# Computing an attention output already transposed, in quadrants of 32 rows

## The chip, the cores and the metric

The kernel runs on one core of a Trainium2 chip. The metric is the time of one execution on the device in microseconds (us). Three runs of the kernel before gave 1435.74, 1436.57 and 1439.3 us; the median, 1436.57 us, is the time before.

## The reference

Three layers follow one another. The first is a gated linear attention over 4 batches, 8 heads, 768 steps and 48 channels; its output, with the heads side by side, is a matrix of 3072 tokens by 384 features. The other two are mixtures on each token.

```python
f = 1.0 / (1.0 + np.exp(-f_logit))
for t in range(S):
    state = f[:, :, t, :, None] * state + np.einsum('bhd,bhe->bhde', k[:, :, t], v[:, :, t])
    y[:, :, t] = np.einsum('bhd,bhde->bhe', q[:, :, t], state)
x = y.transpose(0, 2, 1, 3).reshape(B * S, H * D)
h = x @ w_in                                   # 384 -> 2048
g = (a0 + a1*h + a2*h**2 + a3*h**3) / (1 + abs(b0)*abs(h) + abs(b1)*h**2 + 1e-6)
x = g @ w_out                                  # 2048 -> 384
for e in range(4):                             # 384 -> 1024 -> 384
    out += p[:, e:e+1] * (np.maximum(x @ w1[e], 0) @ w2[e])
```

## The kernel before

The time axis is cut into six chunks of 128 steps, and each chunk into four blocks, one for each batch: 24 blocks. A block of attention works on four pairs of heads; a pair's two heads stand on partitions 0 to 47 and 64 to 111. All chunks of the first mixture after the first, and all of the second, multiply in a split form: a value is a high and a low part, and each product takes three matmuls of 512 columns (`mm_in`, line 836, and `mm_out`, line 846). These are called the main matmuls here. The attention itself uses plain f32, which the profile shows as two records for one product.

One block goes through these steps. Its scores are eight products of k and q, one for each head (`scores`, line 464); VectorE multiplies them by the mask into the two tiles am (`masked`, line 475). k is transposed (`k_t`, line 480) and copied by ScalarE. The output y, tokens on partitions and 384 features on columns, is summed in one bank: for each pair a product of q with the state (`inter`, line 493, weights q, 96 columns of state streaming), and for each head a product of am with v (`intra`, line 488, weights am, 48 columns of v streaming). ScalarE copies y out of the bank (`y_copy`, line 508), TensorE transposes it in three parts (`x_t`, line 511), and ScalarE copies the result into the first mixture's input x as its high part (`x_hi`, line 520); VectorE subtracts to get the low part (`x_lo`, line 525). In the meantime `update` (line 504) multiplies k and v, and `finish` (lines 527 to 538) renews the state for the next chunk. Chunk 0 has no `inter` and no low part.

The order of the work is written out by hand. `fused` walks over steps v; a step holds one expert slice of the second mixture (nine main matmuls in, nine out) and in some steps slices of the first mixture. `Att.stage` says what a block does in its steps k = 1 to 7, and `Att.t0` when a block begins. Two of its lists are fillers: PA is spread among the nine main matmuls of the slice's input product, PB among the nine of its output product (`fill_run` and `fill_step`, one entry of the list at a time). In chunks 1 to 5 the products for y are fillers of PB in step 5; the transposes x_t are fillers in step 6 (chunk 1) or 7 (later chunks). REST is what comes after the step's matmuls. The four blocks of chunk 0 go through `Att.first`, ahead of the second mixture, beside the conversion of the first mixture's weights on VectorE and ScalarE; after it, the first chunk's mixture is computed in f32 (`fill_in`, line 874, and `fill_out`, line 881). Loads of q, k, f and v go through SP's queue. v is loaded in step 2 of a block, 128 rows of 384 numbers.

Of the kernel before, what the change touches and what calls it, by code (L numbers as in the profile page):

```python
# [8 lines left out]
F32 = mybir.dt.float32  # L9
# [8 lines left out]
NB, NH, S, D = 4, 8, 768, 48  # L18
DM = NH * D
C = 128  # L20
NCH = S // C
NP = NH // 2
PR = 112
# [2 lines left out]
NJ2 = 8  # L26
NSLOT = NJ1 + NE * NJ2
SW = 2 * DM
RING = 16
CONV = (-6, -5, -4, -4, -3, -2, -2, -1, 0, 1, 2, 3, 4, 5, 6, 7)  # L30
WARM = (14, 3, 6)
# [307 lines left out]
PA, PB, ACT0, ACT1, POOL1, DVE1, REST = range(7)  # L339
# [57 lines left out]
class Block:  # L397


    def __init__(self, att, c, b):  # L400
        self.att, self.nc, self.c, self.b = att, att.tc.nc, c, b
        if c == 0:
            self.pa, self.pk, self.py = att.bank_sets[b % 2]
            self.px = self.pk
        elif c == 1:
            self.pa, self.pk, self.py = att.bank_sets[0]
            self.px = self.pk
        else:
            self.pa, self.py = self.pk, self.px = att.pair
        self.last = c == NCH - 1  # L410

    def load(self, i):
        t = self.att.p2.tile([128, NP, C], F32, tag="qkf"[i], name="qkf"[i])
# [1 line left out]
        setattr(self, "qkf"[i], t)  # L415

    def load_v(self):
        self.v = self.att.p2.tile([128, DM], F32, tag="v", name="v")
        self.nc.sync.dma_start(out=self.v, in_=self.att.aps["v"][self.b, self.c * C:(self.c + 1) * C, :])

    def exp(self):
# [61 lines left out]
        self.kt = self.att.p1.tile([128, NP, PR], F32, tag="kt", name="kt")  # L483
        self.nc.scalar.copy(out=self.kt, in_=self.pk.rearrange("p (r c) -> p r c", r=NP)[:, :, 0:PR])

    def intra(self, r, a):
        o = (2 * r + a) * D
        self.nc.tensor.matmul(self.py[:, o:o + D], self.am[a][:, r], self.v[:, o:o + D],  # L488
                              start=(self.c == 0 and r == 0 and a == 0), stop=(r == NP - 1 and a == 1))

    def inter(self, r):
        o = 2 * r * D
        self.nc.tensor.matmul(self.py[:, o:o + 2 * D], self.q[0:PR, r], self.att.st[self.b][0:PR, r],  # L493
                              start=(r == 0), stop=False)

    def y_parts(self, *rs):
        fs = []
        for r in rs:
            fs += ([partial(self.inter, r)] if self.c else []) + [partial(self.intra, r, a) for a in range(2)]
        return fs  # L500

    def update(self, r):
        o = 2 * r * D
        self.nc.tensor.matmul(self.pa[0:PR, o:o + 2 * D], self.kt[:, r], self.v[:, o:o + 2 * D], start=True, stop=True)  # L504

    def y_copy(self):
        self.y = self.am[0].rearrange("p r t -> p (r t)")[:, 0:DM]
        self.nc.scalar.copy(out=self.y, in_=self.py[:, 0:DM])

    def x_t(self, m):  # L510
        self.nc.tensor.transpose(self.px[:, m * C:(m + 1) * C], self.y[:, m * C:(m + 1) * C], self.att.consts[2])

    def x_part(self, i):
        x = self.att.x_of(self.c)
# [1 line left out]
        return x[:, :, self.b * C:(self.b + 1) * C]  # L516

    def x_hi(self):
        xt = self.px[:, 0:DM].rearrange("p (m t) -> p m t", m=3)
        self.nc.scalar.copy(out=self.x_part(0), in_=xt)  # L520

    def x_lo(self):
        if self.c:
            xt = self.px[:, 0:DM].rearrange("p (m t) -> p m t", m=3)
            self.nc.vector.tensor_tensor(out=self.x_part(1), in0=xt, in1=self.x_part(0).bitcast(F32), op=ALU.subtract)

    def finish(self):
# [13 lines left out]
class Att:  # L541
# [41 lines left out]
    def first(self, s, conv):  # L583

        new, old, nxt = (self.blocks.get((0, b)) for b in (s, s - 1, s + 1))
        rs = range(NP)
        if s == 0:
            new.exp()
            self.warm(WARM[0])
        if old:  # L590
            old.k_copy()
        if new:
            new.w()
            new.scans()
            new.inverse()
            new.k_hat()
        if nxt:
            nxt.exp()
        for f in conv[0]:
            f()  # L600
        if old:
            old.masked()
            for f in old.y_parts(*rs):
                f()
            for r in rs:
                old.update(r)
        if new:
            new.newton1()
            new.newton2()
            new.q_hat()  # L610
        if old:
            old.y_copy()
            for m in range(3):
                old.x_t(m)
            old.x_hi()
        if new:
            self.warm(WARM[1])
            for r in rs:
                new.scores(r)
            for r in rs:  # L620
                new.k_t(r)
            self.warm(WARM[2])
        for f in conv[1]:
            f()
        if old:
            old.finish()
        if s + 2 < NB:
            blk = self.blocks[0, s + 2] = Block(self, 0, s + 2)
            for i in (2, 1, 0):
                blk.load(i)  # L630
        if old and s + 1 < NB:
            self.blocks[0, s + 1].load_v()
# [14 lines left out]
    def stage(self, blk, k):  # L647
        rs = range(NP)
        if k == 1:
            return {ACT0: [blk.exp], DVE1: [blk.w], REST: [blk.scans]}  # L650
        if k == 2:
            return {ACT0: [blk.inverse], POOL1: [blk.k_hat], DVE1: [blk.newton1], REST: [blk.newton2]}
        if k == 3:
            return {POOL1: [blk.q_hat]}
        if k == 4:
            return {PA: [blk.all_scores] + [lambda: None] * (8 * (blk.c == 1)), REST: [blk.masked]}
        keys = [] if blk.last else [partial(blk.k_t, r) for r in rs]
        upd = [] if blk.last else [partial(blk.update, r) for r in rs]
        copy = [] if blk.last else [blk.k_copy]
        end = ([] if blk.last else [blk.finish]) + [blk.x_lo]  # L660
        xt = [partial(blk.x_t, m) for m in range(3)]
        if blk.c == 1:
            if k == 5:
                return {PB: keys + blk.y_parts(*rs), REST: copy}
            if k == 6:
                return {PA: upd, ACT1: [blk.y_copy], PB: xt, REST: [blk.x_hi] + end}
            return {}
        if k == 5:
            return {PB: keys + blk.y_parts(*rs), REST: copy}
        if k == 6:  # L670
            return {PA: upd, ACT1: [blk.y_copy]}
        if k == 7:
            return {PA: xt, ACT1: [blk.x_hi], REST: end}
        return {}

    def begin(self, v):
        ops = tuple([] for _ in range(7))
        for c in range(1, NCH):
            for b in reversed(range(NB)):
                k = v - self.t0(c, b)  # L680
                if 1 <= k <= 7:
                    for at, fs in self.stage(self.blocks[c, b], k).items():
                        ops[at].extend(fs)
        return ops
# [477 lines left out]
def gla_moe_kernel(tc, qkf, v, vt, w1, w2, ab, probs, ident_d, mask_d, out):  # L1162
    nc = tc.nc
    aps = {"qkf": qkf, "v": v, "vt": vt, "w1": w1, "w2": w2, "out": out}
    with (
# [14 lines left out]
        xs = dp.tile([DM, NB, S], F32, name="xs")  # L1180
# [35 lines left out]
        with tc.If(rv == 0, preferred_fallthrough_block=False):  # L1216
            scan_attention(tc, aps, xs)

            def load_x(g, dst):
                for m in range(3):  # L1220
                    nc.sync.dma_start(out=dst[:, m, :].rearrange("p (b t) -> p b t", b=NB),
                                      in_=xs[m * 128:(m + 1) * 128, :, g * C:(g + 1) * C])
            plain_ffn(tc, aps, consts, load_x)


# [3 lines left out]
def _pack(inputs):  # L1229
    import numpy as _np  # L1230

    def pairs(a, pad):
        a = a.reshape(NB, NP, 2, NCH, C, D).transpose(3, 0, 2, 5, 1, 4)
        return _np.concatenate([a, a[:, :, :, 0:16] if pad else _np.zeros_like(a[:, :, :, 0:16])], axis=3).reshape(
            NCH, NB, 128, NP, C)

    def slots(w_in, w_out):
        f = w_in.shape[1]
        n = f // 128
        a = w_in.reshape(3, 128, n, 128).transpose(2, 1, 0, 3).reshape(n, 128, DM)  # L1240
        return _np.concatenate([a, w_out.reshape(n, 128, DM)], axis=2)

    w1 = slots(inputs['moe_w_in'], inputs['moe_w_out'])
    w2 = [slots(inputs['moe2_w1'][e], inputs['moe2_w2'][e]) for e in range(NE)]
    return {
        'qkf': _np.stack([pairs(inputs['q'], 0), pairs(inputs['k'], 0), pairs(inputs['f_logit'], 1)], axis=3),
        'v': inputs['v'].transpose(0, 2, 1, 3).reshape(NB, S, DM),
        'vt': inputs['v'].transpose(0, 1, 3, 2),
        'w1': _np.ascontiguousarray(w1).view(_np.int64),
        'w2': _np.concatenate(w2, axis=0),  # L1250
        'ab': _np.tile(_np.concatenate([inputs['moe_a'], inputs['moe_b']])[None, :], (128, 1)),
        'probs': inputs['moe2_domain_probs'].reshape(NB, NCH, 128, NE).transpose(2, 1, 0, 3).reshape(128, NCH * NB, NE),
        'ident': _np.eye(128, dtype=_np.float32),
        'mask': _np.triu(_np.ones((128, 128), dtype=_np.float32)),
    }
# [23 lines left out]
```

## Time and profile before

| what | value |
| --- | --- |
| median of three runs | 1436.57 us |
| the profiled execution's own time | 1440.86 us |
| its span, first to last instruction | 1439.0 us |
| PE busy | 1378.3 us (96%) |
| weight loads (PEld) busy | 1105.8 us (77%) |
| VectorE (DVE) busy | 904.4 us (63%) |
| ScalarE (ACT) busy | 674.4 us (47%) |
| GpSimd (POOL) busy | 287.4 us (20%) |
| DMA | 287.80 MB, 200 GB/s |
| share of the chain that ended last | PE 75%, DVE 14%, DMA 3% |

PE stands for TensorE's matmuls and PEld for its weight loads, which overlap them. Matmuls are pipelined: the duration of one row contains its passage through the array, so the pitch between starts, not the duration, is what a matmul takes of a stream. A row with a count joins neighbours of one line; its duration runs from the first start to the last end. A bracket behind a row says how long the engine was idle before it and what ended that.

### The profile page before, as it was taken

Reading aid. Unit: us, or ns where it says so; the run is one execution under the profiler, and the core shown is the slowest. Engines: PE = TensorE matmul, PEld = TensorE weight load, DVE = VectorE, ACT = ScalarE, POOL = GpSimd, SP = SyncE. Lnnn points to the kernel's source line nnn. Section 1 sums busy time; section 2 is a strip of 40 time slices with the busy share of each in tenths; the row PEclk is TensorE's granted clock in tenths of the full one; section 3 lists DMA queues with packets and bytes.
Section 4 is the critical chain, followed back from the end, with each engine's and each line's share of the span. In section 5 each row is a group of like instructions: output and inputs, shape, how many; then the busy total and the mean of one; then the engine's idle time right before and its main releaser. Section 6 shows DMA issues by size and latency. Waiting matters only on the chain.

```text
span 1439.0 us, 18273 instructions
## 1 busy us (share of the span) xinstructions
PE 1378.3 (96%) x6502; PEld 1105.8 (77%) x6502; DVE 904.4 (63%) x1403; ACT 674.4 (47%) x1160; POOL 287.4 (20%) x257
## 2 busy tenths in 40 slices
PE   6898999898989999999999999999999999999996
PEld 6643688686878888887888887888878888888885
DVE  7799844968656657667556676657675655562222
ACT  3577545775635544445454444444444444441111
POOL 0123554556532101112001112001111001111010
PEclk8799999899999999999999999999999999999998
DMA  8244875576766655657566566656556666667650
GB/s 301 91 140 155 284 256 203 207 260 228 279 238 210 215 182 180 208 148 262 174 188 213 167 190 228 204 179 217 193 170 219 195 200 196 193 193 239 194 176 25
DMA packets 115699, 287.80 MB, mean 200 GB/s; under 512 B 13104, under 2 KB 31888, under 8 KB 114832
## 3 DMA queue, kind: packets, MB, share of 16 engines
q1 hardware_dynamic: 115024, 286.36, 61.6%
q8 instruction: 54, 0.88, 0.3%
q14 instruction: 45, 0.37, 0.1%
q10 hardware_dynamic: 576, 0.18, 0.0%
HBM read 237.69 MB, written 48.81 MB: 199 GB/s over the span
## 4 chain that ended last, share of the span: by engine, by line
PE 75%; DVE 14%; DMA 3%; ACT 2%; issue 2%; POOL 2%; SPq 1%; POOLq 0%; ACTq 0%; DVEq 0%
PE bank L846 34%; PE bank L836 32%; PE bank L488 2%; PE bank L464 1%; DMA f<-in_qkf_dram 1%; POOL w L793 1%; DVE y L931 1%; PE bank L493 1%; DVE g L434 1%; PE bank L881 1%; DVE q L910 1%; DVE q L905 1%; PE bank L504 1%; DVE q L919 1%; PE bank L874 1%
## 5 line engine op out<-in xcount | busy, mean ns | idle before, releaser
L836 PE MATMUL bank<-x,w 128*128 128x512 f32 x2448 | 609.2, 395 | 8.0 <-DVE gl L945 6.1
L846 PE MATMUL bank<-gh,w 128*128 128x512 f32 x1632 | 530.6, 401 | 6.0 <-DVE t L981 6.0
L836 PEld LDWEIGHTS bank<-x,w 128*128 128x128 f32 x2448 | 454.1, 189 | 103.0 <-DVE gl L945 7.8
L846 PEld LDWEIGHTS bank<-gh,w 128*128 128x128 f32 x1632 | 305.3, 190 | 68.4 <-DVE t L981 6.9
L846 PE MATMUL bank<-gl,w 128*128 128x512 f32 x816 | 324.9, 398 | 0.0
L945 DVE SCALAR_TENSOR_TENSOR gl<-bank,gh 128x512 fp32r<-128x512 f32 x192 | 131.7, 686 | 136.2 <-ACT gh L944 136.2
L982 POOL TENSOR_TENSOR o<-o,t 128x512 f32<-128x512 f32 x69 | 89.2, 1323 | 512.0 <-DVE t L981 512.0
L846 PEld LDWEIGHTS bank<-gl,w 128*128 128x128 f32 x816 | 154.5, 189 | 30.4
L944 ACT ACTIVATE gh<-bank 128x512 fp32r<-128x512 f32 x192 | 114.0, 594 | 125.9 <-PE bank L836 125.9
L910 DVE SCALAR_TENSOR_TENSOR q<-q,sc,r 128x512 f32<-128x512 f32 x80 | 62.7, 784 | 167.0 <-ACT r L895 167.0
L921 ACT CAST gh<-q 128x512 fp32r<-128x512 f32 x80 | 49.1, 614 | 160.9 <-DVE q L919 160.9
L793 POOL TENSOR_TENSOR w<-rawbuf,w 128x384 fp32r<-128x384 f32 x96 | 104.9, 1120 | 95.6 <-ACT w L792 66.7
L890 ACT COPY h<-bank 128x512 f32<-128x512 f32 x80 | 46.9, 586 | 137.5 <-PE bank L836 137.1
L999 DVE TENSOR_TENSOR s<-s,bank 128x512 f32<-128x512 f32 x45 | 30.7, 683 | 77.8 <-PE bank L846 77.8
L936 DVE TENSOR_TENSOR gl<-q,gh 128x512 fp32r<-128x512 f32 x80 | 55.3, 691 | 35.0 <-ACT gh L921 35.0
L488 PEld LDWEIGHTS bank<-v,am 128*128 128x128 f32 x384 | 65.0, 202 | 12.0 <-DVE am L475 7.9
L911 ACT ACTIVATE r<-q,sc 128x512 f32<-128x512 f32 x80 | 58.0, 725 | 30.9 <-DVE q L910 23.9
L488 PE MATMUL bank<-v,am 128*128 128x48 f32 x384 | 60.6, 264 | 7.5 <-DVE am L475 7.5
L905 DVE SCALAR_TENSOR_TENSOR q<-q,r 128x512 f32<-128x512 f32 x80 | 65.0, 812 | 0.0
L896 ACT ACTIVATE y<-h,sc 128x512 f32<-128x512 f32 x80 | 64.1, 801 | 0.0
L912 ACT ACTIVATE r<-r 128x512 f32<-128x512 f32 x96 | 60.7, 632 | 3.1
L931 DVE SCALAR_TENSOR_TENSOR y<-y,sc,h 128x512 f32<-128x512 f32 x80 | 60.2, 752 | 2.8
(103 smaller groups left out, 1393.3 us busy)
## 6 DMA issues: line engine op xcount, KB each, us to landing
w<-ws SPq DMA_DIRECT2D x448, 384.0 KB, 3.6
ws<-w SPq DMA_DIRECT2D x96, 384.0 KB, 4.1
raw<-in_w_dram SPq DMA_DIRECT2D x16, 768.0 KB, 7.0
rawbuf<-in_w_dram SPq DMA_DIRECT2D x64, 192.0 KB, 3.6
f<-in_qkf_dram SPq DMA_DIRECT2D x24, 256.0 KB, 3.9
k<-in_qkf_dram SPq DMA_DIRECT2D x24, 256.0 KB, 4.0
q<-in_qkf_dram SPq DMA_DIRECT2D x24, 256.0 KB, 4.2
w1s<-wf SPq DMA_DIRECT2D x16, 384.0 KB, 3.7
```

Of the source, the lines that this page charges most:

```text
L488: self.nc.tensor.matmul(self.py[:, o:o + D], self.am[a][:, r], self.v[:, o:o + D], start=(self.c == 0 and r == 0 and a == 0), stop=(r == N ...
L793: nc.gpsimd.tensor_tensor(out=t[:, 1], in0=r, in1=t[:, 0].bitcast(F32), op=ALU.subtract)
L836: nc.tensor.matmul(ps, a[:, o], b[:, kk, :], start=(n == 0), stop=(n == 8))
L846: nc.tensor.matmul(acc[m], a[:, o], b, start=(start and n == 0), stop=(stop and n == last))
L896: nc.scalar.activation(out=y, in_=h, func=AF.Identity, scale=sc[:, 0:1], bias=sc[:, 1:2])
L905: vec.scalar_tensor_tensor(out=q0, in0=q0, scalar=QC, in1=r0, op0=ALU.add, op1=ALU.mult)
L910: vec.scalar_tensor_tensor(out=q, in0=q, scalar=sc[:, 5:6], in1=r, op0=ALU.mult, op1=ALU.add)
L912: nc.scalar.activation(out=r, in_=r, func=AF.Exp, scale=-1.0)
L931: vec.scalar_tensor_tensor(out=y, in0=y, scalar=sc[:, 2:3], in1=h, op0=ALU.subtract, op1=ALU.mult)
L944: nc.scalar.activation(out=gh, in_=h, func=AF.Relu)
L945: nc.vector.scalar_tensor_tensor(out=gl, in0=h, scalar=0.0, in1=gh.bitcast(F32), op0=ALU.max, op1=ALU.subtract)
L982: nc.gpsimd.tensor_tensor(out=o[c][:, m], in0=o[c][:, m], in1=t, op=ALU.add)
```

## The change

The output is computed with features on partitions and tokens on columns. Now the state and v are the weights, and q and am stream. An output lies in column groups of 128 tokens (three of them, n), and in four quadrants of 32 partitions. Group n holds on partitions 0 to 95 the 96 features of pair n, and on partitions 96 to 127 the n-th third of pair 3. The rows of the first mixture's input weights are permuted alike on the host. The state's part takes six products: three with 96 columns of weights, three with 32. The part within the chunk takes four pieces of 32 weight columns for each pair, 16 in all, written quadrant after quadrant. A quadrant in which two heads of 48 meet takes a piece of each, with zeros beside it; v carries these pieces as 256 more columns. Copy, transposes and their step fall away; x_hi goes to step 5 and x_lo to step 6. The list PB now has the inter products as one entry and the intra pieces as another, with two empty entries before and behind.

```diff
+VW = DM + 64 * NP
...
-        self.v = self.att.p2.tile([128, DM], F32, tag="v", name="v")
+        self.v = self.att.p2.tile([128, VW], F32, tag="v", name="v")
...
-    def intra(self, r, a):
-        o = (2 * r + a) * D
-        self.nc.tensor.matmul(self.py[:, o:o + D], self.am[a][:, r], self.v[:, o:o + D],
-                              start=(self.c == 0 and r == 0 and a == 0), stop=(r == NP - 1 and a == 1))
-
-    def inter(self, r):
-        o = 2 * r * D
-        self.nc.tensor.matmul(self.py[:, o:o + 2 * D], self.q[0:PR, r], self.att.st[self.b][0:PR, r],
-                              start=(r == 0), stop=False)
...
+    def y_out(self, quads, n, rows, left, right, stop=False):
+
+        self.nc.tensor.matmul(self.py[32 * quads[0]:32 * quads[-1] + 32, n * C:(n + 1) * C], left[rows], right[rows],
+                              start=not self.begun[quads[0]], stop=stop)
+        for i in quads:
+            self.begun[i] = True
+
+    def inter(self):
+
+        st, rows = self.att.st[self.b], slice(0, PR)
+        for r in range(3):
+            self.y_out((0, 1, 2), r, rows, st[:, r], self.q[:, r])
+            self.y_out((3,), r, rows, st[:, 3, 32 * r:32 * r + 32], self.q[:, 3])
+
+    def intra(self):
+
+        pieces = [[] for _ in range(4)]
+        for r in range(NP):
+            o, z = 2 * r * D, DM + 64 * r
+            for k, (col, a) in enumerate(((o, 0), (z, 0), (z + 32, 1), (o + 64, 1))):
+                quad = (0, 1, 1, 2)[k]
+                pieces[3 if r == 3 else quad].append((quad if r == 3 else r, col, a, r))
+        for i in range(6):
+            for quad in (1, 0, 2, 3):
+                if i < len(pieces[quad]):
+                    n, col, a, r = pieces[quad][i]
+                    self.y_out((quad,), n, slice(0, C), self.v[:, col:col + 32], self.am[a][:, r],
+                               i == len(pieces[quad]) - 1)
+
+    def y_parts(self):
+        return ([self.inter] if self.c else []) + [self.intra]
...
-    def y_copy(self):
-        self.y = self.am[0].rearrange("p r t -> p (r t)")[:, 0:DM]
-        self.nc.scalar.copy(out=self.y, in_=self.py[:, 0:DM])
-
-    def x_t(self, m):
-        self.nc.tensor.transpose(self.px[:, m * C:(m + 1) * C], self.y[:, m * C:(m + 1) * C], self.att.consts[2])
...
-            old.y_copy()
-            for m in range(3):
-                old.x_t(m)
             old.x_hi()
...
+        wait = [lambda: None] * 2
         if k == 5:
-            return {PB: keys + blk.y_parts(*rs), REST: copy}
+            keys = [] if blk.last else [partial(blk.k_t, r) for r in rs]
+            copy = [] if blk.last else [blk.k_copy]
+            return {PB: keys + wait + blk.y_parts() + wait, REST: copy + [blk.x_hi]}
         if k == 6:
-            return {PA: upd, ACT1: [blk.y_copy]}
-        if k == 7:
-            return {PA: xt, ACT1: [blk.x_hi], REST: end}
+            upd = [] if blk.last else [partial(blk.update, r) for r in rs]
+            return {PA: upd, DVE1: [blk.x_lo], REST: [] if blk.last else [blk.finish]}
```

A fallback branch, `plain_ffn` with `load_x`, reads its input in the new order of rows; it is taken only where the decay leaves the safe range.

## Rows read from the trace of the kernel before

**Rows 1.** Busy time by stretch: us, then busy us (instructions) of each engine, PEclk, DMA share, GB/s

```profile
0.00:62.00 62.00, 45.99 (x293) 42.81 (x294) 44.20 (x95) 22.39 (x36) 1.69 (x8) 0.78 0.60 219
...
260.00:480.00 220.00, 204.72 (x980) 166.30 (x980) 159.06 (x222) 125.95 (x233) 99.98 (x89) 0.95 0.68 232
...
700.00:920.00 220.00, 217.51 (x1072) 179.50 (x1072) 141.25 (x218) 102.78 (x174) 29.37 (x26) 1.00 0.62 196
```

**Rows 2.** Timeline, PE, chunk 3: start us, us, engine, line, operation, tiles, shapes, count

```profile
702.09 4.24 PE L836 MATMUL bank<-x,w 128*128 128x512 f32 x18
706.17 0.62 PE L846 MATMUL bank<-gh,w 128*128 128x512 f32 x2
...
726.57 2.20 PE L836 MATMUL bank<-x,w 128*128 128x512 f32 x9
...
729.79 0.73 PE L846 MATMUL bank<-gh,w 128*128 128x512 f32 x2
730.36 0.40 PE L846 MATMUL bank<-gl,w 128*128 128x512 f32 x1
```

**Rows 3.** Timeline, PE, one block's output and its transposes

```profile
736.05 0.39 PE L846 MATMUL bank<-gh,w 128*128 128x512 f32 x1
736.28 0.35 PE L480 MATMUL bank<-ident,k 112*128 112x112 f32 x2
...
736.72 0.36 PE L480 MATMUL bank<-ident,k 112*128 112x112 f32 x2
...
741.92 0.34 PE L504 MATMUL bank<-v,kt 128*112 128x96 f32 x2
...
748.96 0.27 PE L511 MATMUL bank<-ident,am 128*128 128x128 f32 x1
...
749.76 0.27 PE L511 MATMUL bank<-ident,am 128*128 128x128 f32 x1
```

**Rows 4.** Timeline, weight loads (PEld) of the same stretch

```profile
726.35 2.00 PEld L836 LDWEIGHTS bank<-x,w 128*128 128x128 f32 x9
728.70 0.97 PEld L464 LDWEIGHTS bank<-q,k 48*128 48x128 f32 x16 [0.35 <-issue]
...
737.27 0.30 PEld L488 LDWEIGHTS bank<-v,am 128*128 128x128 f32 x2
```

**Rows 5.** Groups by shape: y_copy, with count, busy us, mean ns, idle before

```profile
L508 ACT COPY am<-bank 128x384 f32<-128x384 f32 x24 | 11.4, 476 | 16.0 <-PE bank L488 16.0
```

**Rows 6.** Timeline, PE, start of the fill: f32 weights, 512 columns

```profile
62.93 2.74 PE L874 MATMUL bank<-x,wf 128*128 128x512 f32 x6
```

**Rows 7.** Timeline, PE, two windows inside the scores (728.65 to 728.75, 728.90 to 728.98)

```profile
728.70 0.38 PE L464 MATMUL bank<-q,k 48*128 48x128 f32 x2
...
728.70 0.49 PE L464 MATMUL bank<-q,k 48*128 48x128 f32 x4
```

**Rows 8.** Busy time by stretch, in the start (columns as in rows 1)

```profile
40.00:52.00 12.00, 12.00 (x66) 11.55 (x66) 10.92 (x22) 4.03 (x7) 0.00 (x0) 0.50 0.22 74
```

**Rows 9.** Timeline, PE: rows with waits (idle before, and its releaser, in brackets)

```profile
38.55 0.90 PE L511 MATMUL bank<-ident,am 128*128 128x128 f32 x3 [2.35 <-ACT am L508]
...
60.14 2.84 PE L874 MATMUL bank<-x,wf 128*128 128x512 f32 x6 [0.57 <-ACT x L520]
...
400.84 4.21 PE L836 MATMUL bank<-x,w 128*128 128x512 f32 x9 [4.84 <-DVE gl L945]
...
1069.75 0.46 PE L493 MATMUL bank<-s,q 112*128 112x96 f32 x2 [1.30 <-DVE am L475]
```

**Rows 10.** Timeline, ScalarE and VectorE, waits in the start

```profile
12.21 0.63 ACT L423 ACTIVATE f<-f 112x512 f32<-112x512 f32 x1 [4.38 <-DMA f<-in_qkf_dram]
...
54.90 1.29 DVE L475 TENSOR_TENSOR am<-bank,mask 128x512 f32<-128x512 f32 x2 [2.95 <-PE bank L464]
```

**Rows 11.** DMA issues: v, with count, KB each, median us to landing

```profile
v<-in_v_dram SPq DMA_DIRECT2D x24, 192.0 KB, 4.3
```

More of the change, by code (lines that the diff above doesn't have):

```diff
@@ L401, in __init__ @@
         self.att, self.nc, self.c, self.b = att, att.tc.nc, c, b
[L402 to L407, printed above, removed]
-        else:
-            self.pa, self.py = self.pk, self.px = att.pair
+        if c < 2:
+            self.pa, self.pk, self.py = att.bank_sets[b % 2 if c == 0 else 0]
+        else:
+            self.pa, self.py = att.pair
+            self.pk = self.pa
         self.last = c == NCH - 1
+        self.begun = [False] * 4
     def load(self, i):
@@ L484, in k_copy @@
         self.nc.scalar.copy(out=self.kt, in_=self.pk.rearrange("p (r c) -> p r c", r=NP)[:, :, 0:PR])
-    def intra(self, r, a):
-        o = (2 * r + a) * D
-        self.nc.tensor.matmul(self.py[:, o:o + D], self.am[a][:, r], self.v[:, o:o + D],
-                              start=(self.c == 0 and r == 0 and a == 0), stop=(r == NP - 1 and a == 1))
-    def inter(self, r):
-        o = 2 * r * D
-        self.nc.tensor.matmul(self.py[:, o:o + 2 * D], self.q[0:PR, r], self.att.st[self.b][0:PR, r],
-                              start=(r == 0), stop=False)
[L496 to L500, printed above, removed]
+    def y_out(self, quads, n, rows, left, right, stop=False):
[23 more added lines that the diff above has]
+        return ([self.inter] if self.c else []) + [self.intra]
     def update(self, r):
@@ L518, in x_hi @@
     def x_hi(self):
-        xt = self.px[:, 0:DM].rearrange("p (m t) -> p m t", m=3)
+        xt = self.py[:, 0:DM].rearrange("p (m t) -> p m t", m=3)
         self.nc.scalar.copy(out=self.x_part(0), in_=xt)
@@ L523, in x_lo @@
         if self.c:
-            xt = self.px[:, 0:DM].rearrange("p (m t) -> p m t", m=3)
+            xt = self.py[:, 0:DM].rearrange("p (m t) -> p m t", m=3)
             self.nc.vector.tensor_tensor(out=self.x_part(1), in0=xt, in1=self.x_part(0).bitcast(F32), op=ALU.subtract)
@@ L602, in first @@
             old.masked()
-            for f in old.y_parts(*rs):
+            for f in old.y_parts():
                 f()
@@ L656, in stage @@
             return {PA: [blk.all_scores] + [lambda: None] * (8 * (blk.c == 1)), REST: [blk.masked]}
[L657 to L663, printed above, removed]
-                return {PB: keys + blk.y_parts(*rs), REST: copy}
-            if k == 6:
-                return {PA: upd, ACT1: [blk.y_copy], PB: xt, REST: [blk.x_hi] + end}
-            return {}
+        wait = [lambda: None] * 2
         if k == 5:
-            return {PB: keys + blk.y_parts(*rs), REST: copy}
+            keys = [] if blk.last else [partial(blk.k_t, r) for r in rs]
+            copy = [] if blk.last else [blk.k_copy]
+            return {PB: keys + wait + blk.y_parts() + wait, REST: copy + [blk.x_hi]}
         if k == 6:
-            return {PA: upd, ACT1: [blk.y_copy]}
-        if k == 7:
-            return {PA: xt, ACT1: [blk.x_hi], REST: end}
+            upd = [] if blk.last else [partial(blk.update, r) for r in rs]
+            return {PA: upd, DVE1: [blk.x_lo], REST: [] if blk.last else [blk.finish]}
         return {}
@@ L680, in begin @@
                 k = v - self.t0(c, b)
-                if 1 <= k <= 7:
+                if 1 <= k <= 6:
                     for at, fs in self.stage(self.blocks[c, b], k).items():
@@ L1220, in load_x @@
                 for m in range(3):
-                    nc.sync.dma_start(out=dst[:, m, :].rearrange("p (b t) -> p b t", b=NB),
-                                      in_=xs[m * 128:(m + 1) * 128, :, g * C:(g + 1) * C])
+                    for lo, hi, row in ((0, 96, m * 96), (96, 128, 288 + m * 32)):
+                        nc.sync.dma_start(out=dst[lo:hi, m, :].rearrange("p (b t) -> p b t", b=NB),
+                                          in_=xs[row:row + hi - lo, :, g * C:(g + 1) * C])
             plain_ffn(tc, aps, consts, load_x)
@@ L1241, in slots @@
         return _np.concatenate([a, w_out.reshape(n, 128, DM)], axis=2)
-    w1 = slots(inputs['moe_w_in'], inputs['moe_w_out'])
+    rows = _np.concatenate([_np.r_[96 * m:96 * m + 96, 288 + 32 * m:320 + 32 * m] for m in range(3)])
+    v = inputs['v'].transpose(0, 2, 1, 3)
+    z = _np.zeros_like(v[:, :, 0::2, 0:16])
+    pad = _np.concatenate([v[:, :, 0::2, 32:48], z, z, v[:, :, 1::2, 0:16]], axis=3)
+    w1 = slots(inputs['moe_w_in'][rows], inputs['moe_w_out'])
     w2 = [slots(inputs['moe2_w1'][e], inputs['moe2_w2'][e]) for e in range(NE)]
@@ L1246, in _pack @@
         'qkf': _np.stack([pairs(inputs['q'], 0), pairs(inputs['k'], 0), pairs(inputs['f_logit'], 1)], axis=3),
-        'v': inputs['v'].transpose(0, 2, 1, 3).reshape(NB, S, DM),
+        'v': _np.concatenate([v.reshape(NB, S, DM), pad.reshape(NB, S, 256)], axis=2),
         'vt': inputs['v'].transpose(0, 1, 3, 2),
```

## The prediction

> **What bounds the kernel now.** I read the page's busy shares first and then the busy times by stretch [rows 1]. From 160 us on PE is busy nearly throughout (217.51 of 220 us between 700 and 920) at the full granted clock, while VectorE has 141.25 and ScalarE 102.78 us of the same stretch: there the end of the kernel is the sum of what TensorE must stream. Only the start (0 to 62 us) and the stretch 260 to 480 hold idle PE. Of the 24 blocks of attention, 20 (chunks 1 to 5) lie inside that saturated stream, so the question is what one block's output costs TensorE before and after.
>
> The unit is the main matmul: 18 of them take 706.17 - 702.09 = 4.08 us, or 0.2267 us each [rows 2]. Everything squeezed between them is read as the time beyond that pitch.
>
> **What goes.** In the stretch 736.05 to 741.92 us [rows 3] there are 12 main matmuls (12 x 0.2267 = 2.72 us), four transposes of k and one block's 4 inter and 8 intra products; beyond the main ones it takes 5.87 - 2.72 = 3.15 us. Two transposes of k lie between 736.28 and 736.72 beside one main matmul: (0.44 - 0.23) / 2 = 0.11 us each, 0.43 us for four. The 12 products so cost 2.72 us, 24 records (an f32 product shows as two) of 0.11 us. That is not streaming, since a score with 128 columns takes no longer (below), but the weight load: two loads of 128 columns with nothing between them take 0.30 us where one takes 0.19, so they begin 0.11 us apart [rows 4]. The three transposes x_t cost (749.76 - 748.96) - 3 x 0.2267 = 0.12 us each [rows 3], 0.36 us. **Removed: 2.72 + 0.36 = 3.08 us of TensorE per block.** The ScalarE copy y_copy (0.476 us, 24 times [rows 5]) goes too; behind the main stream it costs the end nothing, because ScalarE is idle half the time [rows 1].
>
> **What comes.** Per block now 3 inter products of 96 output rows, 3 of 32 output rows, and 16 intra pieces of 32 output rows, all streaming 128 columns. Six records that stream 512 f32 columns take 2.74 us with the last one's tail [rows 6], 0.46 us or a little less each, so one of 128 columns takes a quarter, 0.11 us, whatever its weights' width. The six inter products: 12 x 0.11 = 1.32 us, if they don't overlap.
>
> The intra pieces lie in four column quadrants. The nearest row is the scores, two heads on different rows of the array: two matmuls begin together, the next two 0.11 us later [rows 7], and 16 weight loads take 0.97 us, eight pairs of 0.11 us [rows 4]. So pieces on different parts of the array do run together, fully. That is by rows; for columns no row shows it. I take full overlap: quadrant 1 has six pieces and is the longest queue, 6 x 2 x 0.11 = 1.32 us. The bounds are that and no overlap, 32 x 0.11 = 3.52 us.
>
> Cutting the array has its own price. The scores as a whole: the nine main matmuls ahead end their pitch at 726.57 + 9 x 0.2267 = 728.61, and the third matmul after them starts at 730.36, two pitches after 729.91 [rows 2]. Of these 1.30 us the pairs take 0.88; 0.42 us remain for two changes, **0.21 us a change**. It shows as a weight load that waits 0.35 us for "issue" ahead of the scores, where a main matmul's load starts 0.22 us ahead of its matmul (726.35 and 726.57) [rows 2, 4]. Of the 0.21 us, 0.11 are the 128-column load that nothing hides, and 0.10 the draining. With loads in proportion to columns (0.03 for 32, 0.08 for 96) a change costs 0.13 into 32 columns, 0.18 into 96, 0.21 into 128.
>
> The Trainium skill (TensorEngine Tiling (Array Packing), Key Properties) says that changing the tiling mode, and not only the tile, drains the engine. The scores agree with it at 0.21 us; that 96 and 32 output rows are two such modes is no row's to show, and by the rule they would be.
>
> Counting changes per block: the inter loop alternates 96 and 32 rows, three changes in and two back (3 x 0.13 + 2 x 0.18 = 0.75 us). The filler list then has `inter` and `intra` as two entries (10 entries over 9 main matmuls), so a main matmul comes between: 0.21 back, 0.13 in, 0.21 out at the end, 0.55 us. Eight changes, 1.30 us; the bounds are 0 and 8 x 0.21 = 1.68 us. **Added: 1.32 + 1.32 + 1.30 = 3.94 us, against 3.08: +0.86 us per block, x 20 = +17.2 us.**
>
> **What takes some of it back.** In the start the granted clock is 0.50, which is 1.2 GHz, from 40 to 52 us, where PE is busy all the time [rows 8]. There PE waited 2.35 us for y_copy [rows 9], queued on ScalarE behind the conversion; later VectorE waits 2.95 us for the scores [rows 10], and the first matmul of the fill, at 60.14, waits 0.57 us for the last block's copy of x [rows 9], which itself follows y_copy and x_t. Without copy and transposes the scores of the third block come up to 3.8 us sooner, but the masked product behind them still waits for VectorE; I count 0.5 us there, 0.9 at the next block, 1.0 at the last: -2.4 us. Against it v grows from 192 [rows 11] to 320 KB a block, and the first lies ahead of a load that ScalarE waits 4.38 us for [rows 10]: 128 KB at the 219 GB/s of that stretch [rows 1] would be 0.6 us, of which I take 0.4. Net -2 us, bounds -4 to +1. The count of loads on SP's queue stays the same; the later ones of v are issued three steps ahead of use, each step at least 18 main matmuls or 4.1 us, against 4.3 us to landing [rows 11]: hidden. In 260 to 480 PE waits for VectorE anyway (4.84 us once [rows 9]); two of the four blocks there are absorbed, -1.5 us, bounds -3.4 to 0. In the last chunk PE waits 1.30 us for the mask [rows 9]; two empty entries now precede the products: -1 us, bounds -1.3 to 0. The copy x_hi moves a step forward, to the end of the step of the products; behind it on ScalarE stands the next relu, which needs a later matmul, so nobody waits. x_lo and the state's update move a step forward on VectorE with their sum unchanged, behind a PE that is the later one: nothing. The permuted weight rows are packed on the host; the fallback's loads are in a branch that this run doesn't take.
>
> **Sum:** 17.2 - 2.0 - 1.5 - 1.0 = +12.7 us on the profiled execution's 1440.86 (1439.0 span and 1.9 around it). That execution is 4.3 us above the median of the three runs, 1436.57, to which I add the same: **1449 us**.
>
> **The rivals.**
> 1. *Changes cost nothing among column tiles, or 96 and 32 rows run side by side.* Then 2.64 against 3.08 us, -0.44 x 20 = -8.8, with -3 from start and last chunk: **1425, faster**. It decides below 0.08 us a change (break-even 0.64 us a block). For it: the trace has no change of columns. Against: the scores' 0.21 us, both ways. Chance 0.20.
> 2. *Half price:* draining without an exposed load, 0.10 us a change, 0.8 a block: +0.36 x 20 - 4 = **1440**, no change that can be told. Chance 0.13.
> 3. *Less overlap.* If pieces start in the order written, each with its two records one after the other, a piece costs 0.11 us behind its neighbour and the two last of quadrant 1 cost 0.22: 18 x 0.11 = 1.98 us, +0.66 x 20: **1462**. Against: the scores' first two matmuls start together, before the first head's second record [rows 7]. The Trainium skill (TensorE: Matmul & The Clock Gate, Part 3, The mechanism) has matmuls start strictly in order, and loads hidden only behind other row groups; the main stream's loads are hidden behind the same rows [rows 2, 4], so the trace speaks against the second half. Chance 0.13.
> 4. *No overlap of quadrants, the change not doing what its order suggests:* 3.52 for 1.32, +2.2 x 20: **1493**. Chance 0.06.
>
> **How the numbers follow.** The forecast has 0.45 (its own range, from the bounds of changes and absorption, 1443 to 1457); 0.03 is for what I don't see. A measurement of this kernel tells 0.3% (4.3 us) from no change. Faster: rival 1 and some of the rest, 0.23. Same: rival 2 and an edge, 0.14. Slower: 0.63. The range 1426 to 1463 leaves out rival 4, the faster half of rival 1 and little else.
>
> **What would show it.** In the changed profile: weight loads of the inter products, each after a wait for "issue"; intra matmuls four together, 1.3 us from first to last; a stretch of k transposes and products 1.3 us longer than 5.87, with no transposes after it (-0.36). The first main matmul of the fill should start near 58 us, not 60.14. Wrong if four quadrants follow one another at 0.11 us a record, or if 96-row and 32-row products start in one pitch.

## The result, and the profile after

The changed kernel takes 1451.66 us (median of four runs, 1449.26 to 1452.21), the kernel before, run beside it, 1436.15: a ratio of 1.0106 with a 95% interval of 1.0078 to 1.0134, or 15.5 us more. The forecast was 1449 us and slower; the sign and the mechanism hold, and the time lies in the forecast's own range. Two terms of the sum, the gains in the start and between 260 and 480 us, do not hold; the traces show what stood in the start's place.

The profiled execution took 1451.21 us, with a span of 1449.4. The busy times by stretch, as in [rows 1]:

```profile
260.00:480.00 220.00, 200.00 (x1035) 157.92 (x1035) 159.61 (x222) 125.58 (x229) 101.01 (x89) 0.98 0.68 232
...
700.00:920.00 220.00, 217.99 (x1130) 175.68 (x1130) 139.07 (x215) 101.69 (x171) 29.59 (x27) 1.00 0.63 197
```

PE is as busy as before (217.99 of 220 us against 217.51), VectorE and ScalarE slightly less. In this stretch nothing waits more: it is the same stream and has more in it. From 260 to 480 us PE is busy 4.7 us less than in [rows 1], at a granted clock of 0.98 instead of 0.95; the section on the prediction comes back to that stretch. The timeline of PE for one block of chunk 3, which answers to [rows 3]:

```profile
743.30 0.39 PE L842 MATMUL bank<-gh,w 128*128 128x512 f32 x1
...
745.13 2.17 PE L487 MATMUL bank<-q,s 112*96 112x128 f32 x12
747.22 0.50 PE L842 MATMUL bank<-gh,w 128*128 128x512 f32 x1
747.66 1.50 PE L487 MATMUL bank<-am,v 128*32 128x128 f32 x32
749.08 0.50 PE L842 MATMUL bank<-gh,w 128*128 128x512 f32 x1
749.42 0.39 PE L842 MATMUL bank<-gl,w 128*128 128x512 f32 x1
749.65 0.86 PE L832 MATMUL bank<-x,w 128*128 128x512 f32 x3
750.35 0.34 PE L519 MATMUL bank<-v,kt 128*112 128x96 f32 x2
```

From 743.30 to 750.35 there are again 12 main matmuls and four transposes of k, and the block's products: 7.05 - 2.72 = 4.33 us beyond the main ones, against 3.15 before. That is +1.18 us, less the 0.36 us of the three transposes that no longer follow: +0.82 us a block, where 0.86 was forecast.

The 32 records of the intra part take 1.50 us including the last one's tail; one at a time they would need 3.5. The quadrants do run side by side, and four records begin within 0.04 us (a window that ends at 747.68):

```profile
747.66 0.32 PE L487 MATMUL bank<-am,v 128*32 128x128 f32 x4
```

The weight loads of the same stretch, as in [rows 4], show where the time goes instead:

```profile
744.90 0.68 PEld L487 LDWEIGHTS bank<-q,s 112*96 112x96 f32 x4
745.77 0.53 PEld L487 LDWEIGHTS bank<-q,s 112*96 112x96 f32 x4 [0.20 <-issue]
746.50 0.53 PEld L487 LDWEIGHTS bank<-q,s 112*96 112x96 f32 x4 [0.20 <-issue]
747.22 0.19 PEld L842 LDWEIGHTS bank<-gh,w 128*128 128x128 f32 x1 [0.20 <-issue]
747.65 1.23 PEld L487 LDWEIGHTS bank<-am,v 128*32 128x32 f32 x32 [0.25 <-issue]
749.08 0.19 PEld L842 LDWEIGHTS bank<-gh,w 128*128 128x128 f32 x1 [0.20 <-issue]
```

Each bracket is a load that could not go ahead: before 96 columns, before 128, before 32, before 128. (Each of the first three rows joins two loads of 96 and two of 32 columns, so the change inside it has no bracket.) With those three, eight changes lie in one block. The first load of 96 columns, at 744.90, follows a main matmul's 128 columns without a bracket: from 128 to 96 columns no change shows.

### The profile page after: what moved, and what is told of

The parts are those of the page before. It is cut to its first block, busy times and chain, and to the rows that moved or that the text cites. A ratio compares the mean times of both kernels' runs of the same rounds, so it can differ in the third digit from the quotient of the medians.

```text
span 1449.4 us, 19037 instructions
## 1 busy us (share of the span) xinstructions
PE 1379.1 (95%) x6894; PEld 1081.3 (75%) x6894; DVE 907.4 (63%) x1403; ACT 665.3 (46%) x1136; POOL 290.3 (20%) x257
## 4 chain that ended last, share of the span: by engine, by line
PE 76%; DVE 15%; DMA 2%; ACT 2%; issue 2%; POOL 2%; SPq 0%; POOLq 0%; DVEq 0%; ACTq 0%
PE bank L842 34%; PE bank L832 32%; PE bank L487 5%; DMA f<-in_qkf_dram 2%; DVE y L927 1%; PE bank L463 1%; DVE g L433 1%; DVE q L906 1%; POOL w L789 1%; DVE q L915 1%; PE bank L877 1%; PE bank L519 1%; DVE q L901 1%; DVE y L925 1%; DVE t L739 1%
## 5 line engine op out<-in xcount | busy, mean ns | idle before, releaser
L832 PE MATMUL bank<-x,w 128*128 128x512 f32 x2448 | 602.2, 393 | 12.9 <-DVE gl L941 10.8
L842 PE MATMUL bank<-gh,w 128*128 128x512 f32 x1632 | 519.7, 396 | 5.9 <-DVE t L977 5.9
L842 PE MATMUL bank<-gl,w 128*128 128x512 f32 x816 | 320.6, 393 | 0.0
L789 POOL TENSOR_TENSOR w<-rawbuf,w 128x384 fp32r<-128x384 f32 x96 | 108.0, 1150 | 105.6 <-ACT w L788 83.0
L433 DVE TENSOR_TENSOR_SCAN g<-f,sc 112x128 f32<-112x128 f32 x96 | 63.3, 718 | 0.5
L915 DVE SCALAR_TENSOR_TENSOR q<-y,sc,q 128x512 f32<-128x512 f32 x80 | 62.5, 781 | 1.8
```

The lines of the kernel that those rows point to most:

```text
L433: self.nc.vector.tensor_tensor_scan(g[:, r], f[:, r], lim, 1.0, ALU.mult, ALU.min)
L789: nc.gpsimd.tensor_tensor(out=t[:, 1], in0=r, in1=t[:, 0].bitcast(F32), op=ALU.subtract)
L832: nc.tensor.matmul(ps, a[:, o], b[:, kk, :], start=(n == 0), stop=(n == 8))
L842: nc.tensor.matmul(acc[m], a[:, o], b, start=(start and n == 0), stop=(stop and n == last))
L915: vec.scalar_tensor_tensor(out=q0, in0=y0, scalar=sc[:, 3:4], in1=q0, op0=ALU.subtract, op1=ALU.mult)
```

## The experiments

All ran beside the kernel before; ratios are to that.

**e1: the order of the inter products.**

```diff
         for r in range(3):
             self.y_out((0, 1, 2), r, rows, st[:, r], self.q[:, r])
+        for r in range(3):
             self.y_out((3,), r, rows, st[:, 3, 32 * r:32 * r + 32], self.q[:, 3])
```

> The changed kernel with the six inter products in another order: the three of 96 columns first, then the three of 32, so that four of the eight changes of width fall away; the same products, weights and streams. If a change of width costs what the changed kernel's trace shows (0.12 us into 32 columns, 0.17 us back into 96), a block loses 2 x 0.12 + 2 x 0.17 = 0.58 us, 20 blocks 11.6 us: about 1440 us, some 0.3% above the kernel before. If the extra time comes from the number and length of the products, or from the larger loads of v, the order doesn't matter: 1451 us, ratio 1.010.

Measured: 1440.37 us, ratio 1.0023 (1.0006 to 1.0039); 11.3 us less than the changed kernel for four changes a block. With the same 22 products and the same loads of v, only the order differs, so the number of products and the larger loads are out as causes of these 11.3 us. In its timeline the inter part takes 1.59 us where it took 2.17:

```profile
736.42 1.59 PE L487 MATMUL bank<-q,s 112*96 112x128 f32 x12
737.94 0.50 PE L843 MATMUL bank<-gh,w 128*128 128x512 f32 x1
738.38 1.50 PE L487 MATMUL bank<-am,v 128*32 128x128 f32 x32
```

The difference, 0.58 us, is the sum that was written down for two changes into 32 columns and two back.

**e2: inter and intra as one entry of the filler list.**

```diff
     def y_parts(self):
-        return ([self.inter] if self.c else []) + [self.intra]
+        def both():
+            if self.c:
+                self.inter()
+            self.intra()
+        return [both]
```

(and the order of e1.)

> As e1, and inter and intra are one entry of the filler list, so that no main matmul comes between them: two more changes fall away (0.20 us out and 0.12 us in), two are left of eight. By the price of changes another 0.32 us a block, 6.5 us: about 1433.5 us, ratio 0.998. If only the alternation inside inter costs, it stays at e1's time; if the order doesn't matter at all, 1451 us.

Measured: 1426.70 us, ratio 0.9936 (0.9914 to 0.9958). That is 13.7 us less than e1 where 6.5 were expected; the order alone now makes the kernel faster than before. The price of two changes accounts for half. The timeline shows the other half:

```profile
727.64 1.26 PE L487 MATMUL bank<-q,s 112*96 112x128 f32 x9
728.64 0.31 PE L487 MATMUL bank<-am,v 128*32 128x128 f32 x3
728.74 0.27 PE L487 MATMUL bank<-q,s 112*32 112x128 f32 x1
728.77 0.28 PE L487 MATMUL bank<-am,v 128*32 128x128 f32 x3
728.85 0.27 PE L487 MATMUL bank<-q,s 112*32 112x128 f32 x1
```

Inter records of 32 columns (quadrant 3) alternate with groups of three intra records (quadrants 1, 0 and 2) within one step of 0.11 us. Once nothing of another width lies between them, the three narrow inter products run for the most part beside the intra pieces: quadrant 3's queue of 3 + 4 pieces is the longest, 7 x 0.22 = 1.53 us, where inter's narrow part and intra took 0.65 + 1.31 one after the other. That is 0.43 us a block, 8.7 us in all; with the changes 15 us are accounted for against 13.7 measured.

**e3: all of the inter part in quadrants.**

```diff
-        for r in range(3):
-            self.y_out((0, 1, 2), r, rows, st[:, r], self.q[:, r])
-            self.y_out((3,), r, rows, st[:, 3, 32 * r:32 * r + 32], self.q[:, 3])
+        for n in range(3):
+            for i in (1, 0, 2, 3):
+                r, t = (3, n) if i == 3 else (n, i)
+                self.y_out((i,), n, rows, st[:, r, 32 * t:32 * t + 32], self.q[:, r])
```

(and one entry, as in e2.)

> As e2, but the 96-column inter products are cut into quadrants too: 12 inter pieces of 32 columns, four quadrants side by side, then the 16 intra pieces, all in one width; two changes a block. If four quadrants run fully side by side also for the inter part, it takes 3 x 2 x 0.11 = 0.65 us instead of 1.31, the block 0.65 + 1.31 + 0.32 = 2.28 us against 3.08 before: 20 x -0.80 and 3 to 4 us of the start, about 1418 us, ratio 0.987. If 28 pieces in a row are limited by their issue or by their weight loads instead, the inter part takes as long as its 24 records one after the other (2.6 us): 1455 us or more.

Measured: 1421.98 us, ratio 0.9906 (0.9873 to 0.9938): right in kind, 4 us short in size. The block takes what was expected: 728.89 - 726.14 less two main matmuls are 2.30 us, where 2.28 was written down.

```profile
726.14 0.40 PE L847 MATMUL bank<-gh,w 128*128 128x512 f32 x1
726.47 0.86 PE L487 MATMUL bank<-q,s 112*32 112x128 f32 x24
727.14 1.48 PE L487 MATMUL bank<-am,v 128*32 128x128 f32 x32
728.55 0.50 PE L847 MATMUL bank<-gh,w 128*128 128x512 f32 x1
728.89 0.39 PE L847 MATMUL bank<-gl,w 128*128 128x512 f32 x1
```

Twenty-four inter records need 0.67 us to the start of the next part. Counted too much were the 3 to 4 us of the start, which e6 to e9 take up, and something in the blocks: against e8, matmul by matmul, the 20 blocks together gave 13.1 us of the expected 16, and those between 260 and 480 us only 1.6 of 3.2. Why those gave less stays open. Quadrant 1 now holds nine pieces and the others six and seven: the last records run alone.

**e4: the thirds dealt out so that every quadrant holds seven pieces.**

```diff
...
+        for t in range(3):
+            for i in range(4):
+                r = (i + 1 - t) % 4
+                self.y_out((i,), t, rows, st[:, r, 32 * t:32 * t + 32], self.q[:, r])
...
+        for k in range(4):
+            for i in range(4):
+                t, a = (0, 1, 1, 2)[k], k // 2
+                r = (i + 1 - t) % 4
+                o, z = 2 * r * D, DM + 64 * r
+                col = (o, z, z + 32, o + 64)[k]
+                self.y_out((i,), t, slice(0, C), self.v[:, col:col + 32], self.am[a][:, r], k == 3)
...
-    rows = _np.concatenate([_np.r_[96 * m:96 * m + 96, 288 + 32 * m:320 + 32 * m] for m in range(3)])
+    rows = _np.concatenate([(i + 1 - m) % 4 * 96 + 32 * m + _np.arange(32) for m in range(3) for i in range(4)])
```

> As e3, with the twelve thirds of a pair's features dealt out anew, so that each quadrant holds one third in which two heads meet and two whole ones: seven pieces in each quadrant (three inter, four intra) where e3 has nine, six, six and seven; the rows of the first mixture's input weights are permuted to match. If the longest quadrant's queue sets the time at 2 x 0.11 us a piece, a block falls from 9 x 0.22 = 1.96 to 7 x 0.22 = 1.53 us, 20 blocks by 8.7 us: about 1413 us against 1422 for e3, ratio 0.984. If the rate of issue or the weight loads of 56 records in a row set it, it stays at 1422 us; if four streams of 128 columns kept up only while quadrants ran dry, it is slower than e3.

Measured: 1412.76 us (1411.58 to 1413.95), ratio 0.9839 (0.9821 to 0.9858), 9.2 us less than e3 where 8.7 were expected. From the first product to the next main matmul the part takes 1.67 us (719.05 to 720.72) instead of e3's 2.08 (726.47 to 728.55): the longest quadrant's queue sets its time. This version beats both kernels.

```profile
719.05 0.86 PE L487 MATMUL bank<-q,s 112*32 112x128 f32 x24
719.73 1.06 PE L487 MATMUL bank<-am,v 128*32 128x128 f32 x32
720.72 0.50 PE L842 MATMUL bank<-gh,w 128*128 128x512 f32 x1
```

**e5: the intra pieces quadrant after quadrant.**

```diff
-        for i in range(6):
-            for quad in (1, 0, 2, 3):
+        for quad in (1, 0, 2, 3):
+            for i in range(6):
```

The lines with a minus are the changed kernel's: it writes its pieces in turns, one from each quadrant. The words "quadrant after quadrant" in the section on the change mean these turns; here they mean all of one quadrant before the next.

> The changed kernel with the intra pieces written quadrant after quadrant (all six of quadrant 1, then three of 0, three of 2, four of 3) instead of taking turns. Same pieces, same eight changes. If overlap needs neighbours on different quadrants, most pieces run one after the other: 32 records of 0.11 us are 3.5 us instead of 1.31, up to 2.2 us a block, up to 1495 us; two quadrants can still overlap where they meet, so 1480 to 1495. If TensorE starts whatever quadrant is free, however far behind in the queue, it stays at 1451 us. If quadrants never overlapped, it would also stay, and the pieces in the trace would stand 0.11 us apart in both.

Measured: 1471.34 us, ratio 1.0246 (1.0213 to 1.0279): 19.7 us more than the changed kernel, between the two expectations. Overlap needs pieces of other quadrants close by in the order, though TensorE does look some way ahead. Three windows of its timeline, each a row that joins what starts by the window's end:

```profile
705.75 0.30 PE L487 MATMUL bank<-am,v 128*32 128x128 f32 x1
...
705.75 1.06 PE L487 MATMUL bank<-am,v 128*32 128x128 f32 x8
...
705.75 1.20 PE L487 MATMUL bank<-am,v 128*32 128x128 f32 x10
```

Up to 706.60 there are eight records in steps of 0.11 us, one at a time, of the twelve that quadrant 1 has; by 706.70 there are ten. Records of one quadrant stand 0.11 us apart, so the ninth brought one of the next quadrant with it. The whole part takes 2.46 us against 1.50.

**e6 and e7: the old chain of the start with the new products.**

```diff
+            y = old.am[0].rearrange("p r t -> p (r t)")[:, 0:DM]
...
+            nc.scalar.copy(out=y, in_=old.py[:, 0:DM])
+            for m in range(3):
+                nc.tensor.transpose(old.pk[:, m * C:(m + 1) * C], y[:, m * C:(m + 1) * C], self.consts[2])
             old.x_hi()
```

(e6; in e7 the last line gives way to a copy of x from old.pk.)

> The changed kernel with the four blocks of chunk 0 given back a copy by ScalarE and three transposes ahead of their copy of x (they write where nothing is read afterwards), so that the start has the old chain with the new products; blocks of chunks 1 to 5 as in the changed kernel. If copy and transposes were what the start lost, the fill's first matmul goes from 56.7 back to 59 to 60 us, and about 2.3 us of it reach the end: 1454 us against 1451.7. If the start gained by the products themselves, or by a higher granted clock, it stays near 57 us and 1451.7.

Measured: 1450.51 us, ratio 1.0104 (1.0081 to 1.0126); the fill starts at 55.46 us, earlier than without copy and transposes. The expectation that the old chain's return costs 2.3 us falls. The fill's first matmul in the changed kernel and in e6:

```profile
56.73 2.77 PE L870 MATMUL bank<-x,wf 128*128 128x512 f32 x6
```

```profile
55.46 2.74 PE L875 MATMUL bank<-x,wf 128*128 128x512 f32 x6
```

> As e6, and x of chunk 0 is now copied from the bank of the transposes, so that the last block's copy waits for copy and transposes as in the kernel before; chunk 0's x is by this a transposed one, not the reference's. In e6 the fill started at 55.5 us, before the 56.7 of the changed kernel, with a granted clock of 0.81 from 40 to 52 us (0.72 in the changed kernel, 0.50 before). If the old chain's length is what the start lost, the fill now starts at 57 us or later and the whole is 1 us or more above e6 at the same granted clock (0.8 and above from 40 to 52 us); if the granted clock sets it, the start follows the clock, 56 to 57 us at about 0.8, and near 60 us only where it is 0.5.

Measured: 1451.38 us, ratio 1.0100 (1.0072 to 1.0127); the fill starts at 56.20 us, with the same 0.57 us of waiting as in [rows 9], at a granted clock of 0.89 from 40 to 52 us. So the wait for the last block's copy of x moves the fill's start by 0.74 us from e6 to e7. Neither kernel differs from the changed one in its time.

**e8 and e9: the kernel before, profiled again.**

> The kernel before, unchanged, profiled once more, because its executions lie between 1432 and 1441 us and the profile read for the prediction is one of 1440.9. If its start and the stretch from 260 to 480 us are as slow each time, the fill starts at 60 us again at a granted clock of 0.50 from 40 to 52 us. If the clock there differs between executions, an execution of 1433 to 1436 us shows a higher one (0.7 or more in the start, 0.97 in 260 to 480) and a fill at 57 to 58 us, and 4 to 5 us of the change's start are not the change's.

> As e8, a third profile of the kernel before: whether its time follows the granted clock of the start and of 260 to 480 us (lower clock, longer time), or not.

Measured: 1433.66 and 1434.81 us. The fill's first matmul in e8, and the start's busy times (columns as in rows 1) in e8:

```profile
56.08 2.84 PE L874 MATMUL bank<-x,wf 128*128 128x512 f32 x6 [0.57 <-ACT x L520]
```

```profile
40.00:52.00 12.00, 11.89 (x99) 11.01 (x98) 11.74 (x24) 4.84 (x8) 0.00 (x0) 0.81 0.23 76
```

and in e9:

```profile
40.00:52.00 12.00, 11.69 (x98) 10.81 (x98) 11.74 (x24) 4.83 (x8) 0.00 (x0) 0.82 0.22 74
```

The granted clock of that stretch was 0.81 and 0.82, not 0.50 [rows 8], and the fill began at 56.08 and 56.17 us, not 60.14 [rows 9]. The wait of 0.57 us is there all the same. In the stretch 260 to 480 us the clock was 0.97 instead of 0.95. The execution that the prediction was read from (1440.86 us) was near the slow end of what the kernel before does by itself: the 15 executions beside e1 to e3 and e5 lie between 1432.78 and 1441.35 us.

## Why the prediction was right, and where it was not

**What goes: right, and slightly too small.** The 24 records at the pace of their weight loads and the three transposes left; they were read as 3.08 us, and the transposes were 0.06 us dearer (below). e1, e3 and e4 follow from the same numbers to within 4 us; e2 came out 6.8 us faster than written down, for an overlap that had not been counted.

**Streams of 128 columns at 0.11 us a record, four quadrants at once: right.** The intra part took 1.50 us with its tail, the forecast's 1.32 and 0.17 of tail and load. e3 and e4 show it for 56 records in a row; e5 that it is the order by turns that gives it. Rival 4 (1493) would have shown single records throughout, and is out.

**Changes of width: right, and shown.** Forecast were 0.13, 0.18 and 0.21 us, 1.30 us a block. Four changes taken away gave 11.3 us (e1), 0.14 us each on average, against (0.13 + 0.18) / 2 = 0.155. Rivals 1 and 2 (free, 0.10 us) are out. The Trainium skill (TensorEngine Tiling (Array Packing), Key Properties) says that changing the tiling mode drains the engine. The traces agree for changes between 96 or 128 columns and 32, and show none from 128 to 96. The four that e1 removes cost 0.57 us a block (11.3 / 20), most of the whole difference.

**Rival 3, pieces in the order written: out in the changed kernel, and not quite wrong as a rule.** Four records begin together, though as written each piece's second record stands between them. By the rule in the Trainium skill (TensorE: Matmul & The Clock Gate, Part 3, The mechanism), matmuls start strictly in order; e5 shows a limited look past waiting records, not strict order. That loads are hidden only behind other row groups, as the Trainium skill says in the same place, does not hold here: 32 loads in four column quadrants on the same rows take 1.23 us in all, beside the matmuls.

**The start's -2 us: wrong.** This is the failed step. It took 2.35 us of waiting for y_copy and the last block's chain for time that the change would give back. The kernel before has the same wait in e8 (2.37 us) and starts its fill at 56.08 us all the same, 0.65 us before the changed kernel. The 4 us between e8 and the profile that was read come from the granted clock: at 43.4 us the two executions are 0.06 us apart, at the fill 4.06, and in between the same rows take longer in the profile that was read. The 16 records of the third block take 3.49 us there at a granted clock of 0.50 (46.1 to 48.8 us), and 1.99 in e8 at 1.00.

```profile
46.06 3.49 PE L488 MATMUL bank<-v,am 128*128 128x48 f32 x16
```

```profile
45.63 1.99 PE L488 MATMUL bank<-v,am 128*128 128x48 f32 x16
```

What the change did free, PE spent waiting for VectorE. The forecast let the third block's products gain 0.5 us; they begin at 46.14 us, 0.51 us later than in e8, after a wait of 4.97 us for the mask, which VectorE starts at 44.80 us (44.29 in e8) in a row of work without gaps. The changed kernel:

```profile
44.80 1.29 DVE L474 TENSOR_TENSOR am<-bank,mask 128x512 f32<-128x512 f32 x2
...
46.14 2.77 PE L487 MATMUL bank<-am,v 128*32 128x128 f32 x32 [4.97 <-DVE am L474]
...
46.10:48.80 2.70, 2.66 (x32) 2.09 (x32) 2.67 (x5) 0.04 (x1) 0.00 (x0) 0.50 0.00 0
```

Behind that wait the granted clock is 0.50, and the products take 2.77 us instead of 1.50. In e6, where copy and transposes are back, PE waits only 0.33 us there, the clock is 1.00, and the fill starts 1.27 us sooner:

```profile
46.11 1.50 PE L487 MATMUL bank<-am,v 128*32 128x128 f32 x32 [0.33 <-DVE am L474]
...
46.10:48.80 2.70, 2.69 (x44) 2.50 (x45) 2.67 (x5) 2.27 (x4) 0.00 (x0) 1.00 0.00 0
```

**The -1.5 us between 260 and 480 us: wrong too.** Against e8 the distance grows by 3.5 us over the four blocks there and by 3.1 over the next four: nothing was absorbed.

Put together: against e8 the changed kernel's span is 1449.4 - 1431.8 = 17.6 us longer. At the 187th matmul of 512 columns, in the fill and ahead of the first block of chunk 1, it is 2.3 us behind (157.8 against 155.5 us), and by the last one 17.9: 15.6 us over the 20 blocks. At each of the seven blocks between 480 and 885 us the distance grows by 0.75 us: by 1.17 where the products are, less 0.42 where the transposes were. Twenty times that is 15.0, where 17.2 was forecast. Three smaller terms together add 0.5. The four blocks from 260 to 480 us cost 0.5 us more than that. The last chunk's wait for the mask fell from 1.27 us (e8) to 0.60, so 0.7 of the forecast's 1.0 came. And the second block's scores wait 0.98 us for q from GpSimd, where they waited 0.32 in e8; the forecast had nothing for that. The changed kernel's two rows:

```profile
170.64 1.16 PE L463 MATMUL bank<-q,k 48*128 48x128 f32 x16 [0.98 <-POOL q L459]
...
1080.51 2.25 PE L487 MATMUL bank<-q,s 112*96 112x128 f32 x12 [0.60 <-DVE am L474]
```

So the forecast's 17.2 was 2.2 us too much, and of the 4.5 us that it took off again only 0.7 were there: errors of opposite sign. That +12.7 came as near as it did to the measured +15.5 is in part luck.

Open is why the changed kernel falls another 1.7 us behind e8 between the fill's start and the 187th matmul. e1 to e7 pass there between 155.3 and 158.5 us; each of them loses 0.3 to 1.5 us on that way against e8, and e9 none, so a part of it may be the change's. No run separates it.

## What to carry to other kernels

Small products packed into parts of the array pay twice, in streaming and in changes of shape; count the changes, and put all pieces of one shape in one uninterrupted run, in turns over the quadrants and with equal queues. Here the same arithmetic went from 1451.7 us (eight changes, uneven queues) to 1412.8 us (two changes, even queues), from 1% slower to 1.6% faster than the kernel that had no quadrants. And a wait of one engine in the start is no gain to book before it is clear what that engine would wait for next, here VectorE's mask; nor is a stretch that ran at half the clock, until a second profile shows it too.

## What the runs showed that was not expected

Pieces of different products, even with 112 rows in one and 128 in the other, share the array freely as long as all are 32 columns wide (e2). TensorE starts a record past waiting ones of another quadrant, but only past a few: in e5 the first record of the next quadrant started when three of quadrant 1's were still waiting ahead of it, not when four were; by the same count the first records of the other two quadrants each started past four, so no run gives one fixed limit. The granted clock of the start differs from execution to execution of one kernel (0.50, 0.81 and 0.82 from 40 to 52 us), and was worth 4 us of the fill's start. Work taken off TensorE there left it idle before VectorE's mask, and it came back at half the clock (2.77 us for products that take 1.50).
